# Two interleaved layers on one core: VectorE's exponentials begin in the first layer with the 12th head in place of the 11th

## The chip, the cores and the metric

The kernel runs on one core of a Trainium2 chip. The metric is device time in microseconds of one execution, the median over several runs. The engines are TensorE (matmuls, written PE in the profile, its weight loads PEld), VectorE (DVE), ScalarE (ACT), GpSimd (POOL) and SyncE (SP), which issues nearly all DMAs. Each engine runs its own queue in order and waits on semaphores. Matmul results land in PSUM, which has eight banks of 128 partitions x 512 float32; everything else lies in SBUF or in HBM.

## The reference

Two blocks, each applied twice: multi-head attention with 16 heads of 28 features over 2048 tokens, then a gated MLP, each behind a layer norm and with a residual.

```python
def _A_ref(x, wqkv, wo):
    B, S, D = x.shape                      # 1, 2048, 448
    H = 16; Dh = D // H                    # 28
    qkv = (x @ wqkv).reshape(B, S, 3, H, Dh).transpose(2, 0, 3, 1, 4)
    q, k, v = qkv[0], qkv[1], qkv[2]
    scores = jnp.einsum("bhqd,bhkd->bhqk", q, k) * (Dh ** -0.5)
    p = _softmax(scores, axis=-1)
    o = jnp.einsum("bhqk,bhkd->bhqd", p, v)
    return o.transpose(0, 2, 1, 3).reshape(B, S, D) @ wo

def _B_ref(x, w_gate, w_up, w_down):       # F = 1792
    g = x @ w_gate; u = x @ w_up
    return (_sigmoid(g) * u) @ w_down

x = A_x
x = x + _A_ref(_layernorm(x), A_wqkv, A_wo)
x = x + _B_ref(_layernorm(x), B_w_gate, B_w_up, B_w_down)
x = x + _A_ref(_layernorm(x), A_wqkv, A_wo)
x = x + _B_ref(_layernorm(x), B_w_gate, B_w_up, B_w_down)
```

## The kernel before

Each layer runs in four stages, one after the other: `project` makes queries, keys and values; `attend` does the scores, the exponentials and the sums with the values; `out_project` applies `wo`; `gated` is the MLP. Float32 operands are split into two 16-bit parts for the products. The change lies in `attend` (L831), and only in its first call, that of the first layer.

**Units.** The scores of a head form a 2048 x 2048 matrix. It is cut into 16 chunks of 128 keys, and each chunk into 4 units of 128 keys x 512 queries, so 64 units a head and 1024 a layer. `scores` (L856) computes a unit with four matmuls into one PSUM bank. Unit number `u` belongs to head `u // 64`. Heads are counted from 0 in the code, so "the 11th head" is head 10.

**Two ways to an exponential.** Most units go in threes: `score(g)` fills three banks (`triple`, two sets of three in turn, so six of the eight banks) and ScalarE exponentiates all three in one pass of 128x1536 (L871) into one of six `prob` buffers. These are the `main` units, and `g` counts their groups. In heads from `free_from` on, two units a head take a second way: `score_aside` (L873) computes the unit into a single bank, and VectorE makes the exponential with a polynomial and a shift into the exponent, ten instructions from L881 to L890. The table `side` says which: when the unit at chunk 4 of the head has been scored, the unit of chunk 10, query block 3, is done aside; at chunk 9, that of chunk 15, block 1. `free_from` is 10 in the first layer and 0 in the second.

**Mixing.** `mix` (L907) multiplies the probabilities of a chunk with the values and adds into the head's accumulator, a bank of its own (`acc`). A chunk is mixed in four quarters of 128 queries out of each block. After the last chunk, `finish(h)` (L928) copies the accumulator out on VectorE (L933), divides by the sum of the exponentials (L934 to L936), splits the result (L937, L938) and sends it by DMA to the `ot` tiles.

**The two remaining banks.** The accumulator of head `h` has bank `h % 2`. The side units of head `h` use the bank `1 - h % 2`, which is the one that held the accumulator of head `h - 1`. A matmul of a side unit therefore waits until L933 of `finish(h - 1)` has read that bank.

**The order.** It is written out by hand: a loop over `g` scores group `g`, then does at most one side unit that is due, then mixes as many quarters as the pace says (three a group up to `alone`, the group at which head `free_from` begins; after that `pace`, which counts the side units in). Mixing stays at least two groups behind the scores. TensorE executes this order as it stands:

```python
        for g in range(2, groups + 3):
            more(g)
            x = g - 2.25
            due = int(3 * x if x < alone else 3 * alone + (x - alone) * pace)
            ...
            if begin:
                score_aside(begin.popleft())
                done += 1
            while done < due and i < quarters and last_group[i // 4] <= g - 2:
                ...
                mix(i, n)
```

`more(g)` also fetches the operands of a head two ahead (`HeadOperands.load`: a MEMSET on VectorE at L467 and five loads, and one more for the guard rows) when the ninth unit of a head is scored.

**What else VectorE does in this stage.** In the first layer alone, `Prepare` (L715) measures, scales and splits the weights of `wo`, `w_gate`, `w_up` and `w_down` and writes the parts to HBM for both layers. `along` calls it after every sixth chunk that has been mixed; each step reads the next raw weights, writes out the pack made before, and works on the raw weights that have come (L189 and L194 for the splits). It has 26 steps, after the chunks 6, 12, ... 156. The last lies in head 9.

Of the kernel before, what the change touches and what calls it, by code (L numbers as in the profile page):

```python
# [88 lines left out]
def interleaved_layers(ctx: ExitStack, tc: tile.TileContext, x_in, wqkv, wo, w_gate, w_up,  # L89
# [741 lines left out]
    def attend(layer, values, heads, last_values, gate, keep):  # L831
# [8 lines left out]


        side = {}
        free_from = 10 if layer == 0 else 0
        for h in range(free_from, H):
            for at, kc, qb in ((4, 10, 3), (9, 15, 1)):
                side[(h * NT + at) * NB] = (h * NT + kc) * NB + qb
# [320 lines left out]
    for layer in range(LAYERS):  # L1167
        values, heads, last_values = project(layer, wq, first)
        gate = WeightsGated()
        outs = attend(layer, values, heads, last_values, gate, wq.keep)  # L1170
        mlp_first = out_project(outs, gate)
        wq = WeightsQKV()

        def before_next(f, wq=wq):
            if f == 6:
                wq.load()

        first = gated(layer, mlp_first, gate, before_next)
# [28 lines left out]
```

## Time and profile before

| | us |
|---|---|
| median of 3 runs | 2001.17 (1999.59 to 2002.54) |
| the profiled execution, whole | 2000.05 |
| its span, first to last instruction | 1998.3 |
| TensorE busy | 1965.6 (98%) |
| ScalarE busy | 1167.3 (58%) |
| VectorE busy | 1003.4 (50%) |
| scores of the first layer, first pass of ScalarE to last | 126.1 to 591.8 |
| scores of the second layer, the same | 1124.1 to 1568.2 |
| exponential passes of ScalarE (L871) | 669, busy 898.4 |

The profile is one execution, taken by the hardware profiler. Times inside it count from the start of the span. A row of the timeline has the start, the length, the engine, the line in the kernel, the operation, output and inputs, how many instructions were merged, and in brackets how long the engine had been idle before and what ended that. A row of the list of waits has who waited for whom, the total in us, the number of times and the longest. A row of stretches has for each engine the busy time and the number of instructions (PE, PEld, DVE, ACT, POOL), then the clock granted to TensorE (1.00 is full), the busy share of the DMA engines and the GB/s that they moved. Passes of ScalarE overlap by some tenths of a microsecond, so the length of a row is not the spacing of passes; the busy time of a line is the union of its instructions.

### The profile page before, as it was taken

The numbers are of one execution on the slowest core, as the hardware profiler recorded it, in microseconds if no ns is written. First come the engines' busy times: TensorE is split into PE (matmuls) and PEld (weight loads), VectorE is DVE, ScalarE is ACT, GpSimd is POOL, SyncE is SP. The second block draws the span as 40 slices with busy tenths as digits, with TensorE's granted clock in tenths as the row PEclk, the third lists the DMA queues.
The fourth block names the chain that finished last, engine by engine and source line by source line (L and its number), as shares of the span: only waits on it lengthen the run. The fifth ranks groups of instructions, "written<-read, shape, count | busy, mean of one in ns | idle before, by whom it ended". The sixth has DMA issues, their size and how long they took to land. (4 is left out here: it accounts for less than half of the span.)

```text
span 1998.3 us, 48079 instructions
## 1 busy us (share of the span) xinstructions
PE 1965.6 (98%) x21549; PEld 1001.7 (50%) x21549; DVE 1003.4 (50%) x1551; ACT 1167.3 (58%) x1129; POOL 33.5 (2%) x76
## 2 busy tenths in 40 slices
PE   9999999979999999999999999999999999999999
PEld 4445555545554444444444555555555544444444
DVE  6634545477664323333255477677776732323222
ACT  5569999979981211121235699999999412121211
POOL 2000000000000000000000000000000000000000
PEclk9999999989999999999999999999999999999999
DMA  4563544751016101010234311111111250101000
GB/s 166 161 208 84 149 124 152 224 146 43 17 51 233 37 1 37 1 38 1 92 94 140 100 48 32 48 49 44 46 34 51 68 196 11 56 1 56 0 19 19
DMA packets 98633, 153.77 MB, mean 77 GB/s; under 512 B 9584, under 2 KB 79216, under 8 KB 95600
## 3 DMA queue, kind: packets, MB, share of 16 engines
q1 hardware_dynamic: 89728, 146.21, 23.9%
q10 hardware_dynamic: 8688, 4.36, 0.9%
q8 instruction: 173, 2.83, 0.6%
q14 instruction: 44, 0.36, 0.1%
HBM read 97.52 MB, written 45.68 MB: 72 GB/s over the span
## 5 line engine op out<-in xcount | busy, mean ns | idle before, releaser
L871 ACT ACTIVATE prob_s<-sc 128x1536 f32<-128x1536 f32 x669 | 898.4, 1562 | 15.4 <-PE sc L856 13.0
L907 PE MATMUL acc<-prob_s,val_s 128*32 128x256 f32 (+3 forms) x7938 | 568.1, 381 | 0.0
L856 PE MATMUL sc<-qp_s 114*32 114x512 f16 x8016 | 557.8, 380 | 3.2 <-ACT val_s L567 1.3
L1116 ACT ACTIVATE sig_q<-gate 128x512 f32<-128x512 f32 x112 | 60.8, 595 | 597.4 <-PE up L386 597.4
L856 PEld LDWEIGHTS <-qp_s 114*32 114x32 f16 x8192 | 247.6, 95 | 251.9 <-issue 142.8
L907 PEld LDWEIGHTS acc<-prob_s,val_s 128*32 128x32 f32 x7938 | 263.2, 110 | 155.1 <-issue 9.7
L1117 DVE SCALAR_TENSOR_TENSOR sig_q<-up,sig_q 128x512 f32<-128x512 f32 x112 | 72.1, 686 | 513.8 <-ACT sig_q L1116 513.8
L1080 PE MATMUL dnp<-dn_s,hhl_q 128*128 128x448 f16 x448 | 158.4, 354 | 0.0
L1081 PE MATMUL dnp<-dn_s,hhl_q 128*128 128x448 f16 x448 | 157.9, 352 | 0.0
L1082 PE MATMUL dnp<-dn_s,hhl_q 128*128 128x448 f16 x448 | 157.9, 352 | 0.0
L372 PE MATMUL qkp<-xhl_s,wqk_s 128*128 128x512 f16 x616 | 139.6, 379 | 2.6 <-ACT xhl_s L178 0.9
L379 PE MATMUL gate<-xhl_s,gu_s 128*128 128x512 f16 x336 | 127.3, 379 | 3.4 <-ACT xhl_s L178 2.5
L380 PE MATMUL gate<-xhl_s,gu_s 128*128 128x512 f16 x336 | 127.3, 379 | 1.4 <-DVE xhl_s L179 1.4
L381 PE MATMUL up<-xhl_s,gu_s 128*128 128x512 f16 x336 | 127.3, 379 | 0.0
L380 PE MATMUL up<-xhl_s,gu_s 128*128 128x512 f16 x336 | 127.3, 379 | 0.0
L379 PE MATMUL up<-xhl_s,gu_s 128*128 128x512 f16 x336 | 127.3, 379 | 0.0
L381 PE MATMUL gate<-xhl_s,gu_s 128*128 128x512 f16 x336 | 127.3, 379 | 0.0
L933 DVE COPY oraw_q<-acc 128x512 f32<-128x512 f32 x32 | 22.1, 692 | 179.1 <-PE acc L907 179.0
L935 DVE RECIPROCAL oden_q<-oden_q 128x512 f32<-128x512 f32 x32 | 107.3, 3353 | 1.1
L380 PEld LDWEIGHTS <-gu_s 128*128 128x128 f16 x672 | 65.7, 98 | 81.3 <-issue 3.9
L381 PEld LDWEIGHTS <-gu_s 128*128 128x128 f16 x672 | 65.7, 98 | 81.3 <-issue 2.5
L379 PEld LDWEIGHTS <-gu_s 128*128 128x128 f16 x672 | 65.7, 98 | 79.0 <-issue 1.7
(139 smaller groups left out, 1900.8 us busy)
## 6 DMA issues: line engine op xcount, KB each, us to landing
qp_s<-qk_scr SPq DMA_DIRECT2D x96, 224.0 KB
qk_scr<-qkhl_q SPq DMA_DIRECT2D x56, 256.0 KB
gu_s<-gu_parts SPq DMA_DIRECT2D x14, 1024.0 KB
xraw_s<-xt_scr SPq DMA_DIRECT2D x14, 768.0 KB
xt_scr<-xs_s SPq DMA_DIRECT2D x38, 224.0 KB
qp_s<-qk_scr SPq DMA_DIRECT2D x64, 112.0 KB
gu_parts<-pack_s SPq DMA_DIRECT2D x7, 1024.0 KB
raw_s<-in_B_w_down_dram SPq DMA_DIRECT2D x6, 896.0 KB
```

The source lines that it names most:

```text
L372: nc.tensor.matmul(pm, w, x, start=(i == 0), stop=(i == len(terms) - 1))
L379: nc.tensor.matmul(pm, wh(o, kt), blk.hi[:, kt, :], start=(kt == 0), stop=False)
L380: nc.tensor.matmul(pm, wh(o, kt), blk.lo[:, kt, :], start=False, stop=False)
L381: nc.tensor.matmul(pm, wl(o, kt), blk.hi[:, kt, :], start=False, stop=False)
L856: nc.tensor.matmul(ps[32 * j:32 * j + 32, :], hd.k[:, keys], hd.q[:, qb * W:(qb + 1) * W], start=True, stop=True, tile_position=(0, 32 * j))
L871: nc.scalar.activation(prob[:, 0:n, :], ps[:, 0:n, :], AF.Exp, scale=exp_scale)
L907: nc.tensor.matmul(acc[qb * VC:(qb + 1) * VC, s], v[:, kc % TB, h, :], probs[c * NB + qb][:, s], start=(kc == 0 and a == 0), stop=(kc == N ...
L935: nc.vector.reciprocal(den, den)
L1080: nc.tensor.matmul(pm, hl[:, 0, s], dw[:, 0, :], start=(f == 0), stop=False)
L1081: nc.tensor.matmul(pm, hl[:, 0, s], dw[:, 1, :], start=False, stop=False)
L1082: nc.tensor.matmul(pm, hl[:, 1, s], dw[:, 0, :], start=False, stop=(f == NF - 1))
L1117: nc.vector.scalar_tensor_tensor(sigs[a], pms[2 * a + 1], PS, sigs[a], op0=ALU.mult, op1=ALU.mult)
```

## The change

In the first layer the heads with side units begin with head 11 in place of head 10. Head 10's two side units (12 side units in the layer before, 10 after) become main units, exponentiated by ScalarE. `alone` and `pace` follow: the pace of three quarters a group holds through head 10, and the pace after that goes from 3.176 to 3.192 units of mixing and side work a group. The second layer is not touched.

```diff
@@ -840,7 +840,7 @@
         side = {}
-        free_from = 10 if layer == 0 else 0
+        free_from = 11 if layer == 0 else 0
         for h in range(free_from, H):
             for at, kc, qb in ((4, 10, 3), (9, 15, 1)):
                 side[(h * NT + at) * NB] = (h * NT + kc) * NB + qb
```

## Prediction

> **What bounds the kernel now.** I read the page's busy rows by slice first, then the waits, then the timeline at the one place where both fall, then stretches of the two attention stages.
>
> ```profile
> span 1998.3 us, 48079 instructions
> ...
> PE   9999999979999999999999999999999999999999
> ...
> DVE  6634545477664323333255477677776732323222
> ACT  5569999979981211121235699999999412121211
> ```
>
> TensorE is full in every slice of 50 us but the ninth (400 to 450 us), and ScalarE falls in the same slice. Everywhere else in both attention stages both are full, so time is gained there only in that slice. The waits name it:
>
> ```profile
> PE aside L856 <- DVE oraw_q L933: 10.3, 1, 10.3
> ...
> ACT prob_s L871 <- PE sc L856: 13.0, 5, 11.4
> ```
>
> One wait of TensorE, once, 10.3 us: the first score unit that VectorE is to exponentiate (`aside`) waits for the copy at L933, and ScalarE then waits 11.4 us for TensorE. The reason is PSUM: the `aside` tile of head 10 lies in bank 1, which is head 9's accumulator, and L933 is what empties it. The timeline at that place (start, length, engine, line):
>
> ```profile
> 422.87 0.75 DVE L189 TENSOR_SCALAR pack_s<-raw_s,up 128x1024 f16<-128x1024 f32 x1 [9.60 <-DMA gu_parts<-pack_s]
> ...
> 427.40 1.76 DVE L467 MEMSET qp_s<- 18x2048 f16 x1 [0.48 <-issue]
> ...
> 429.20 0.69 DVE L933 COPY oraw_q<-acc 128x512 f32<-128x512 f32 x1
> ...
> 429.94 0.62 PE L856 MATMUL aside<-qp_s 114*32 114x512 f16 x4 [10.33 <-DVE oraw_q L933]
> ...
> 431.18 1.52 PE L856 MATMUL sc<-qp_s 114*32 114x512 f16 x12
> ...
> 433.52 0.83 PE L856 MATMUL sc<-qp_s 114*32 114x512 f16 x12
> ```
>
> VectorE runs its queue in order. Head 9's sums were complete on TensorE by about 417.4 (the mixing call that holds them starts at 416.75), but VectorE stood in the last weight split of `Prepare`, which itself stood 9.60 us until an earlier pack had been written out. Its L933 came 12 us late, and TensorE, whose queue is in order too, stood at `aside` with every later score and mixing behind it. The 10 us before that (the MEMSET at 400.72 waits 10.30 us for a `gu_parts` write, so head 8's L933 starts at 402.52) cost nothing, since no `aside` existed then.
>
> ScalarE's timeline prices the whole loss:
>
> ```profile
> 408.96 12.46 ACT L871 ACTIVATE prob_s<-sc 128x1536 f32<-128x1536 f32 x9
> 432.81 1.45 ACT L871 ACTIVATE prob_s<-sc 128x1536 f32<-128x1536 f32 x1 [11.39 <-PE sc L856]
> 434.47 8.34 ACT L871 ACTIVATE prob_s<-sc 128x1536 f32<-128x1536 f32 x6 [0.21 <-PE sc L856]
> ```
>
> The ninth pass ends at 421.42, the sixteenth at 442.81: seven passes took 21.39 us. A pass costs 1.343 us (the page's L871 row: 898.4 us over 669 passes), so seven cost 9.40 and **12.0 us are lost**. That is more than the 10.33 of idle TensorE because the clock fell too:
>
> ```profile
> 420.00:423.00 3.00, 0.00 (x0) 0.00 (x0) 0.13 (x1) 1.42 (x2) 0.00 (x0) 1.00 1.01 423
> 423.00:430.00 7.00, 0.06 (x4) 0.05 (x7) 6.37 (x8) 0.00 (x0) 0.00 (x0) 0.50 0.57 209
> 430.00:433.00 3.00, 3.00 (x32) 1.41 (x35) 2.97 (x2) 0.19 (x1) 0.00 (x0) 0.50 0.85 209
> 433.00:436.00 3.00, 3.00 (x60) 1.61 (x56) 2.90 (x5) 2.73 (x3) 0.00 (x0) 0.95 0.73 158
> ```
>
> The third number from the right is the granted clock: half from 423 to about 433. Some 3.3 us of matmuls ran at half speed after the wait (twelve scores took 1.28 us start to next group, against 0.65 later), which is the other 1.6 us.
>
> **The change, part by part.** *Head 10 loses its two side units.* TensorE no longer asks for bank 1 in head 10. The next reader of that bank is head 11's first mixing, some 28 us later, when L933 of head 9 is long done. VectorE's chain up to 436 us hangs on DMAs and on itself, not on the stalled matmuls, so it stays where it is while TensorE and ScalarE go on under it. Gain: 12.0 us.
>
> *VectorE loses 20 instructions*, two chains of ten, each 6.37 us (435.89 to 442.26 for the first), 12.7 us in all. It is busy 110.4 of the 154 us from 436 to 590, off the path: worth nothing.
>
> *The two units go into the main passes.* Main units of this layer go from 1012 to 1014. That is 338 passes either way, the last with one unit before and three after. TensorE's scores and mixings are the same in number. Cost from both sides:
> - Upper: ScalarE as the bound, two thirds of a pass, 2/3 x 1.343 = 0.9 us.
> - Lower: the number of passes does not change, only the end does. From the last score to the out projection this layer takes 3.35 us (590.74 to 594.09) with one unit in its last pass, the second layer 3.57 (1567.17 to 1570.74) with two: 0.22 a unit, 0.43 for two. Against this, 21 passes move from the mixed pace to the pace without side units: 1.343 (110 passes, 441.33 to 589.09) against 1.339 (55 passes, 153.87 to 227.52), 0.1 less. So 0.3.
> - Between: the passes without side units do 6 units of TensorE work each (3 scores, 3 mixed quarters), those with 6.18; 21 x 0.18 x 1.343/6.18 = 0.8 us of TensorE work is put off, less the same 0.1: 0.7.
> A gain is excluded, as nothing gets less on TensorE or ScalarE. I take 0.6.
>
> *The mixing pace* after the switch goes from 3.176 to 3.192 a pass; the second layer runs at 3.190 in 1.343 us a pass: nothing more than is counted.
>
> *Queues.* No DMA is added or taken away; SP's order is the same, its loads and stores after head 9 only carry other buffers, and POOL has nothing in this stage. Head 11's operands were issued from 400.26 to 404.63 and the DMA share is near zero from 407 to 410, so they have landed by then; they are wanted at about 441 instead of 453. Head 12's, issued by 432, are wanted at about 470.
>
> *The next `aside` is head 11's*, in bank 0, behind L933 of head 10. That copy ran at 457.62; 12.0 earlier is 445.6, done by 446.3. The `aside` comes one pass later against it than before (pass 240, the copy in pass 237): 459.75 - 12.0 + 1.34 = 449.1. That is a margin of 2.8 us, where the other heads show 1.0 to 2.3 and never wait. VectorE ends its last late work at 435.98.
>
> **Sum** against the profiled execution (2000.05 us, span 1998.3): -12.0 + 0.6 = -11.4, so 1988.65. The median shown is 1.1 higher than that execution (2001.17); I put half of that on top: **1989.2 us**.
>
> **The rivals.** *A second late copy.* The wait moves to head 11's `aside`. For it: heads 8 and 9 both had their copy late by DMA waits in front of it. Against: `Prepare` has ended, and only the MEMSET for head 13's operands stands before the copy. Even a repeat of the longest DMA wait (10.30) from 436.0 ends at 446.3, MEMSET 1.77 and copy 0.69 later it is 448.8, still before 449.1. A wait of about 5 us would leave 1989.2 + 5 = 1994.
>
> *The busiest engine decides.* The two stretches with passes show ScalarE busy all the time (157.03 of 157.30 us from 433.7 to 591) and VectorE 112.56. If the 12 us came back elsewhere (an input of the out projection that is late anyway), only the added two units on ScalarE would remain: 2000.05 + 0.9 = 2000.95, no change. Against it: in the list of TensorE's waits the next largest after the 10.3 us is 2.5 us (two waits of a gate product for its split input), so no input later in the span is now waited for, and none is near enough to being late to swallow 12 us that come off everything before it alike. [...]
>
> *Slower.* L933 of head 10 is held up longer than that of head 9 was. One wait of VectorE for a DMA in front of the MEMSET does it: it would have to end after 449.1 + 12.0 + 4 - 2.5 = 462.6, so last 26 us from 436.0, for a time 0.2% up, 2004 or more. The longest such wait seen is 10.3.
>
> **How the numbers follow.** As forecast 0.85; second late copy 0.06 (1994); absorbed 0.05 (2001); slower 0.04 (2005). About 0.2% (4 us) is what a measurement of this kernel tells from no change. Faster: 0.85 and most of the second, 0.89; same 0.07; slower 0.04. The range: low 2000.05 - 12.1 + 0.3 - 0.5 (the fastest run is 0.5 under the profiled one), less a margin, 1987.0; high 2000.05 - 11.5 + 0.9 + 2.5 (the slowest run), 1992.0, and 1.0 towards the second late copy: 1993.0.
>
> **What would show it.** In the profile after: the wait of `aside` for L933 gone and the ninth slice full; no half clock between 420 and 435; the copy of head 9 still at about 429, that of head 10 at about 446; 338 passes of ScalarE in this layer at 1.34 us; L881 in 42 instances, not 44; the out projection at about 583 instead of 594.09. It is wrong if `aside` waits for L933 in head 11, if another wait of TensorE appears between 420 and 460, or if the out projection starts early and the end does not move.

## The result, and the profile after

The changed kernel takes 1989.5 us (median of 5 runs, 1988.37 to 1993.31) against 2000.45 before (5 runs); the ratio is 0.9948, with a 95% interval of 0.9933 to 0.9962. It is faster by 0.5%. The forecast was 1989.2, within 1987.0 to 1993.0. The profiled execution after takes 1989.2 us against 2000.05, its span 1987.5 against 1998.3.

The busy rows by slice of the changed kernel, with the row of the granted clock under them:

```profile
span 1987.5 us, 48026 instructions
...
PE   9999999999999999999999999999999999999999
...
DVE  6634545557764332323265477677766732323222
ACT  5569999999971212121135799999999312121111
...
PEclk9999999999999999999999999999999999999999
```

TensorE's ninth slice is full now, ScalarE's too. In the list of TensorE's waits the 10.3 us for L933 is gone, and nothing has taken its place; these are the two longest:

```profile
PE gate L379 <- ACT xhl_s L178: 2.9, 2, 1.9
PE vp L396 <- PEq L674: 2.0, 2, 1.3
```

The timeline of VectorE around the old wait, and the first side unit of head 11:

```profile
420.41 0.75 DVE L189 TENSOR_SCALAR pack_s<-raw_s,up 128x1024 f16<-128x1024 f32 x1 [9.28 <-DMA gu_parts<-pack_s]
...
426.75 0.69 DVE L933 COPY oraw_q<-acc 128x512 f32<-128x512 f32 x1
...
445.30 0.69 DVE L933 COPY oraw_q<-acc 128x512 f32<-128x512 f32 x1 [9.53 <-PE acc L907]
...
448.43 0.40 PE L856 MATMUL aside<-qp_s 114*32 114x512 f16 x4
```

VectorE is nearly as late with head 9's copy as it was: it stands 9.28 us for the write of a pack (9.60 before) and copies at 426.75. Nobody waits for it. Head 10's copy runs at 445.30, the moment its sums are complete, and the side unit that needs the bank comes 2.44 us after the copy has ended. The same four stretches as before show no idle TensorE and a full clock:

```profile
420.00:423.00 3.00, 3.00 (x68) 1.88 (x64) 2.56 (x3) 3.00 (x3) 0.00 (x0) 1.00 0.50 202
423.00:430.00 7.00, 7.00 (x128) 3.54 (x121) 6.37 (x7) 7.00 (x6) 0.00 (x0) 1.00 0.66 201
430.00:433.00 3.00, 3.00 (x64) 1.70 (x57) 2.90 (x4) 3.00 (x4) 0.00 (x0) 1.00 0.87 186
433.00:436.00 3.00, 3.00 (x56) 1.40 (x51) 2.29 (x2) 3.00 (x3) 0.00 (x0) 1.00 0.08 21
```

For all that follows I compare one stretch, "the stage": from the first pass of ScalarE in the first layer (L871) to the first product of the out projection (L396), read from the timeline. Its first and last rows before, and then after, are:

```profile
126.09 2.79 ACT L871 ACTIVATE prob_s<-sc 128x1536 f32<-128x1536 f32 x2 [2.38 <-DMA qp_s<-qk_scr]
...
594.09 0.36 PE L396 MATMUL op<-wout_s,ot_s 128*128 128x448 f16 x1
```

```profile
125.54 2.79 ACT L871 ACTIVATE prob_s<-sc 128x1536 f32<-128x1536 f32 x2 [1.82 <-DMA qp_s<-qk_scr]
...
582.07 0.36 PE L396 MATMUL op<-wout_s,ot_s 128*128 128x448 f16 x1
```

The stage repeats far better than whole runs. Before it is 468.00 us, after 456.54: **11.46 us less**. The second layer's attention, which is not touched, takes 446.68 and 446.70. The two spans differ by less, 10.8 us: the stretch between the two attentions went from 529.97 to 531.26 (it lies between 528.2 and 532.0 in all runs below but one), and the first pass starts 0.55 sooner.

### The profile page after: what moved, and what is told of

The parts are those of the page before. It is cut to its first block, busy times and chain, and to the rows that moved or that the text cites. A ratio compares the mean times of both kernels' runs of the same rounds, so it can differ in the third digit from the quotient of the medians.

```text
span 1987.5 us, 48026 instructions
## 1 busy us (share of the span) xinstructions
PE 1964.1 (99%) x21533; PEld 1003.5 (50%) x21533; DVE 991.6 (50%) x1531; ACT 1168.0 (59%) x1129; POOL 33.3 (2%) x76
## 5 line engine op out<-in xcount | busy, mean ns | idle before, releaser
L871 ACT ACTIVATE prob_s<-sc 128x1536 f32<-128x1536 f32 x669 | 899.0, 1565 | 3.2 <-DMA qp_s<-qk_scr 2.1
L933 DVE COPY oraw_q<-acc 128x512 f32<-128x512 f32 x32 | 22.1, 692 | 180.4 <-PE acc L907 180.3
```

The source lines that it names most:

```text
L871: nc.scalar.activation(prob[:, 0:n, :], ps[:, 0:n, :], AF.Exp, scale=exp_scale)
```

## The experiments

**Is it the late copy, or the side units themselves?** Four kernels tell these apart (e1, e2, e4 and e5 below). The first two leave the side units where they were, or add some, and make `Prepare` end sooner:

```diff
-            if prepare and prepare.steps and c > 4 and c % 6 == 0:
+            if prepare and prepare.steps and c > 4 and c % 5 == 0:
```

> The kernel before, its side units from head 10 on as they were, but Prepare takes a step after every fifth chunk instead of every sixth, so that its last step lies in head 8 and VectorE is no longer late at head 9's copy. Measure: the first layer's attention stage, from the first pass of ScalarE to the first product of the out projection: 468.0 us before, 456.5 after the change. Theory (VectorE's late copy of head 9 held the side unit of head 10): the wait is gone although no unit is moved, stage about 455.9 us (456.5 less the 0.6 that the pair costs on ScalarE and TensorE), whole about 1988.9 us. Rival (the pair of side units itself is what costs, through VectorE's work or the shared bank): the pair is still there, stage about 468 us, whole about 2000.5 us.

Measured: 1994.45 us, ratio 0.9967 (0.9954 to 0.9981); the stage is 460.14. The side unit of head 10 no longer waits, though both units are still there. The stage is 4.2 us longer than expected, because VectorE is now late one head sooner, so late that the next user of head 7's bank is stopped, the first mixing of head 9 (TensorE's waits, then its timeline):

```profile
PE acc L907 <- DVE oraw_q L933: 2.6, 1, 2.6
```

```profile
389.63 0.41 PE L907 MATMUL acc<-prob_s,val_s 128*32 128x128 f32 x8
392.66 0.64 PE L907 MATMUL acc<-prob_s,val_s 128*32 128x256 f32 x8 [2.62 <-DVE oraw_q L933]
```

ScalarE's passes lose 4.4 us there (start to start, over 1.343 a pass). Without them the stage would be 455.8, and 455.9 was expected.

With the same edit and `free_from = 9` (e2):

> The same earlier Prepare, and side units from head 9 on. Theory: no late copy in front of head 9's side unit either (Prepare ends at chunk 130, the copy of head 8 comes at chunk 143), and one more pair saves 0.3 to 0.9 us: stage about 455.3 us, whole about 1988.3 us. Rival (a pair costs by itself): one pair more than before, so some 11 us slower than before, 2011 us.

Measured: 2000.08 us, ratio 0.9993 (0.9982 to 1.0003), no change; stage 465.00. The forecast missed: the late copy is now that of head 8, and head 9's side unit waits for it. (Head 9's first mixing waits 1.5 us as well, for the copy of head 7.) ScalarE's passes lose 10.1 us there; without them the stage would be 454.9, and 455.3 was expected.

```profile
PE aside L856 <- DVE oraw_q L933: 6.5, 1, 6.5
```

Both misses have one cause: I placed the end of `Prepare` by its last step, and not by how far VectorE lags behind its steps. At one step every five chunks it lags by more than a head, which takes 28.5 us: the copy of head 7 starts at 391.91 in the first of these kernels, and TensorE's last product of that head ends at 360.91, 31.0 us sooner. The rival falls all the same: with one pair more than before the stage is 3 us shorter, not 11 longer.

The third (e4) puts the changed kernel's `Prepare` off by one head, so that its last steps stand before head 10's copy:

```diff
-            if prepare and prepare.steps and c > 4 and c % 6 == 0:
+            if prepare and prepare.steps and c > 20 and (c - 16) % 6 == 0:
```

> The changed kernel (side units from head 11), with all 26 steps of Prepare put off by 16 chunks, one head: its last two steps stand before the copy of head 10 as they stood before the copy of head 9. Theory: the wait comes back, now at head 11's first side unit, with about the same length: stage about 468 us, whole about 2000.9 us. Rival (fewer side units are what gained): units are those of the changed kernel, stage 456.5 us, whole 1989.5 us.

Measured: 2010.64 us, ratio 1.0044 (1.0032 to 1.0056); stage 479.30. The wait is back at head 11, with the changed kernel's own side units, and twice as long. Its waits, then VectorE's timeline:

```profile
PE aside L856 <- DVE oraw_q L933: 20.4, 1, 20.4
```

```profile
457.62 0.75 DVE L189 TENSOR_SCALAR pack_s<-raw_s,up 128x1024 f16<-128x1024 f32 x1 [15.31 <-DMA gu_parts<-pack_s]
...
468.05 0.69 DVE L933 COPY oraw_q<-acc 128x512 f32<-128x512 f32 x1
```

The write that VectorE waits for stands in SyncE's queue behind the stores of head 9. Those are eight and not four, as head 9's features lie in two `ot` tiles, and SyncE issues them from 442.34 to 448.49 before the next loads (to 452.1) and the write. That the stores make up the whole of the further 10 us I did not test.

The fourth (e5) leaves everything in place and lets TensorE come to head 10's side units later:

```diff
-            for at, kc, qb in ((4, 10, 3), (9, 15, 1)):
+            places = ((7, 13, 3), (11, 15, 1)) if layer == 0 and h == 10 else ((4, 10, 3), (9, 15, 1))
+            for at, kc, qb in places:
```

> The kernel before, with head 10's two side units scored later in the head, at chunks 7 and 11 instead of 4 and 9 (they are then the units of chunks 13 and 15). Nothing else moves. Theory: TensorE reaches the side unit three chunks later, 3 x 4/3 x 1.343 = 5.4 us, so it waits about 5 us instead of 10.3, the clock still falls; 6.6 us lost instead of 12.0: stage about 462.6 us, whole about 1995.1 us. Rival (the number of side units decides): stage 468 us, whole 2000.5 us.

Measured: 1997.59 us, ratio 0.9976 (0.9964 to 0.9989); stage 462.66, against 462.6 expected. TensorE's wait (the edit shifts the lines by one):

```profile
PE aside L857 <- DVE oraw_q L934: 4.2, 1, 4.2
```

This is the cleanest of the four: as many units on the same engines, only asked for later (5.5 us, counted from the first pass), and 5.34 us less in the stage. That this meets the forecast to 0.1 us is partly luck. The wait fell by 6.2 us, as the copy came 0.7 sooner too, but the half clock behind it lasted longer (430.30 to 435.24, against 429.94 to 433.29 before), which at half speed costs 0.8 us more, an estimate from these two lengths.

**What a pair of side units is worth.** The changed kernel again, and one with `free_from = 15` (e3):

> The changed kernel once more, beside the three below on one chip. First attention stage 456.5 us as before, whole about 1989.5 us, and the copy of head 9 again at about 427 us with nobody waiting for it.

Measured: 1989.02 us, ratio 0.9944 (0.9927 to 0.9960); stage 456.48, head 9's copy at 427.5 with no one behind it.

> Side units in the first layer from head 15 on: four heads more than in the changed kernel give their pair to ScalarE's passes, and nobody waits for VectorE. Theory (a pair on VectorE saves a little, 0.3 to 0.9 us, of which 0.8 by the stage of e1 less its gaps): stage 457.7 to 460.1 us, 459.6 by the 0.8, whole about 1992.6 us. Rival (side units cost by themselves, so that fewer are better): under 456.5 us.

Measured: 1991.74 us, ratio 0.9957 (0.9943 to 0.9971); stage 461.25, above the 457.7 to 460.1 expected. Of that, 1.07 us lie between the first two passes and the third, where nothing differs in the code: the granted clock was half there, from 125.30 to 128.72, and it was full in the changed kernel. The other 3.64 us over 456.54 are 0.91 for each of four pairs: ScalarE's two thirds of a pass, 0.895, nearly to the figure. Side units on VectorE are worth something, and fewer are not better.

**Why VectorE is late.** Two ways to free it, with the side units from head 10 on as before. One large buffer more, which serves the packs too (e6):

```diff
-N_SLOTS = 19
-N_QUART = 12
+N_SLOTS = 20
+N_QUART = 8
```

> The kernel before with 20 large buffers in place of 19, and 8 small ones in place of 12 to make room. What made VectorE late is open between two: (a) a buffer still being written out to HBM is taken again at once, as there are too few; (b) SyncE's queue issues the writes late, behind stores that wait for VectorE. By (a) the waits of 10.3 and 9.6 us for writes to gu_parts shrink, the copy of head 9 comes at about 418 us, the side unit does not wait: stage about 455.8 us, whole about 1989 us. By (b) both waits stay: stage 468 us, whole 2000.5 us. The fewer small buffers may add waits of VectorE for the stores of a finished head, later in a head, with no one behind them.

Measured: 1993.35 us, ratio 0.9961 (0.9947 to 0.9975); stage 457.81, with 1.75 us of that again before the third pass (half clock from 131.72 to 135.13); without them it would be 456.06, near the 455.8 of (a). The whole misses the 1989 expected because in its profile the first pass starts at 131.43, 5.3 us later than before and ahead of the stage; whether the fewer small buffers cause that I did not test. Another queue for the writes (e7):

```diff
-                nc.sync.dma_start(*self.pack[0:2])
+                nc.gpsimd.dma_start(*self.pack[0:2])
```

> The kernel before with the writes of Prepare's packs issued by GpSimd's queue, which is empty in this stage, in place of SyncE's. By (b), SyncE's order as the cause: a write starts when its pack is ready (the pack of 390.4 at once and not at 395.3; that of 413.3 at once and not behind the stores of head 8), the copy of head 9 comes 5 to 12 us earlier, stage 456 to 463 us, whole 1989 to 1996 us. By (a), too few buffers alone: stage 468 us, whole 2000.5 us.

Measured: 1990.19 us, ratio 0.9954 (0.9937 to 0.9970); stage 456.02. VectorE's timeline, of the kernel with 20 buffers and then of that with the writes on GpSimd's queue:

```profile
418.84 1.76 DVE L467 MEMSET qp_s<- 18x2048 f16 x1 [1.58 <-DMA gu_parts<-pack_s]
424.52 0.69 DVE L933 COPY oraw_q<-acc 128x512 f32<-128x512 f32 x1 [3.91 <-PE acc L907]
```

```profile
412.71 1.76 DVE L467 MEMSET qp_s<- 18x2048 f16 x1 [0.48 <-issue]
418.26 0.69 DVE L933 COPY oraw_q<-acc 128x512 f32<-128x512 f32 x1 [3.79 <-PE acc L907]
```

In both, head 9's copy waits for TensorE and not the other way round. So neither half alone made VectorE late: a pack's buffer is wanted again at once, and its write leaves SyncE late; taking away either is enough. With the writes on GpSimd the stage is 0.52 us shorter than the changed kernel's, with head 10's pair still on VectorE: about what that pair is worth in the changed kernel, if the other queue itself costs nothing.

**Can more side units be had that way?** GpSimd's queue for the writes, and side units from heads 8, 5 and 0 on (in the last two, in heads before 10, the units of chunks 12 and 15, scored at chunks 4 and 8):

> Prepare's packs written from GpSimd's queue, side units from head 8 on. With the writes there, VectorE copied the heads 7, 8 and 9 as soon as TensorE had them, so nobody should wait; two pairs more than with head 10, 0.5 to 0.9 us each: stage 454.2 to 455.0 us against 456.0, whole about 1988.8 us. If VectorE's waits for raw weights (6.6 us in head 8) hold a side unit's result, TensorE waits in the mixing and the stage is over 456 us.

> The same with side units from head 5 on; in the heads before 10 they are the units of chunks 12 and 15, scored at chunks 4 and 8, so that VectorE has longer. Five pairs more than with head 10: stage 451.5 to 453.5 us if VectorE keeps up beside Prepare, whole about 1987 us; over 456 us if it does not.

> The same with side units in all heads of the first layer. Ten pairs more than with head 10: stage 447 to 451 us if VectorE keeps up (the second layer, which has them in all heads and no Prepare, takes 446.7), whole about 1982 to 1985 us; over 456 us if waits for raw weights hold the copies or the results of side units.

Measured: 1989.7 us (stage 456.72), 2005.54 (464.28) and 2001.2 (466.36). All three missed. New waits take more than the pairs bring. From head 8 on they are 1.2 us for a late copy and 1.2 for VectorE's reading of the first side unit; from head 0 on, TensorE's waits read:

```profile
PE aside L857 <- DVE expo_q L882: 7.5, 3, 3.2
PE aside L857 <- DVE oraw_q L934: 6.0, 2, 5.1
```

The kernel with head 5 has a shorter stage than before and is 0.2% slower as a whole (ratio 1.0020, 1.0010 to 1.0030); that from head 0 on is no change (0.9993, 0.9982 to 1.0003). The one with head 5 takes 536.0 us between the two attentions, with one wait of TensorE of 4.5 us among the second layer's values for which the profile names no cause. What causes it is open. No version tried beats the changed kernel by more than the runs can tell: the writes on GpSimd with head 10 (0.9954) or head 8 (1989.7 us, ratio 0.9938, 0.9922 to 0.9955) stand beside its 0.9948.

## Why the prediction was right

*The bound and the wait.* The chain L933 late, bank held, `aside` stopped, everything behind it stopped, is shown by e5 (later request, less loss), e4 (late VectorE put back, wait back) and e7 (VectorE on time, no wait with the units unmoved).

*The gain, 12.0 us.* The prediction took it from ScalarE's passes, with the half clock in it, and not from the 10.33 us of the wait list. The most direct check is e7, which takes the wait away and leaves every unit in place: its stage is 11.98 less than before. In the changed kernel the stage fell by 11.46. Added back, the longer end (0.43) and the passes after head 10, which come every 1.345 us and no longer every 1.343 (110 passes, 0.2), make 12.1.

*The cost, 0.3 to 0.9, taken at 0.6.* The end of the stage is the part that can be read directly: from the start of the last pass to the out projection 2.32 us before (591.77 to 594.09), 2.76 after (579.32 to 582.07), 0.43 more, the figure forecast. The whole is 0.52 by e7's stage. For pairs beyond this one it is 0.91: the changed kernel's two units filled a last pass that was two thirds empty, so its 338 passes stayed 338, while `free_from = 15` needs 341. The upper end of the range was the price of the next pairs, not of this one.

*What stays late.* The prediction said that VectorE's chain up to 436 us hangs on DMAs and not on the stalled TensorE, so that it would stay. The copy moved from 429.20 to 426.75; the repetition had 427.5, and `free_from = 15` 429.73. Of the 2.45 us, 2.15 were there already at head 8's copy (402.52 to 400.37), ahead of anything that the change moves, so this is scatter and not an effect of the change.

*The next side unit.* Forecast: copy done at 446.3, request at 449.1. Measured: 445.99 and 448.43, margin 2.44 where 2.8 was said. The out projection was forecast at about 583 and starts at 582.07.

*The rivals.* The second late copy did not come in the changed kernel, but it is real: e1, e2 and e4 are three ways to it, and of these e4 alone made the kernel slower. One wait of 26 us for a DMA was said to be needed for a slower kernel; with `Prepare` put off, 15.3 us did it. The wait began at 442.31 and not at 436.0, and four weight splits (8.2 us) came between it and the MEMSET, which the forecast had excluded since `Prepare` had ended. The time named for the MEMSET, 462.6, was passed (466.26). Of the rival of the busiest engine only the smaller term came, more work on ScalarE: 0.9 us was taken for it from the passes of this case, and e3 has 0.91 a pair. The gap, 11.39 us on ScalarE before, did not come back elsewhere.

*The sum.* 11.4 us were forecast, 11.46 came in the stage and 10.8 in the span, whose other stretches scatter by more than the difference. That the whole came within 0.3 us of the forecast is luck in part: single runs of the changed kernel lie between 1988.37 and 1993.31, and the 0.55 us put on top of the sum was a compromise between the profiled execution and the median before.

## What to carry to other kernels

Look at what the last buffer of a side job stands behind, not only at how busy its engine is: VectorE was half empty (50% busy), but in order, and a store waiting in another queue held up the one copy that TensorE needed. Here a request moved to behind a late engine's copy was worth more (12.0 us) than the work that moved with it cost (0.5), and a late copy that had no one behind it cost nothing, so first find who asks first. Price a stall by the passes that did not start: here they were worth 12.0 us, for a wait of 10.33 us with the granted clock at half (0.50) until 433.29.

## What the runs showed of the hardware

In these runs the granted clock also fell beside waits far shorter than the 10.3 us of this case. In e1 TensorE stood 2.62 us (390.04 to 392.66), began again at full clock (1.00 from 392.70 to 393.80), and was then at half for 3.4 us. The stretches (the third number from the right is the clock):

```profile
390.00:392.60 2.60, 0.04 (x4) 0.00 (x0) 2.46 (x2) 1.62 (x2) 0.00 (x0) 1.00 0.01 2
392.70:393.80 1.10, 1.10 (x24) 0.62 (x28) 1.06 (x2) 0.00 (x0) 0.00 (x0) 1.00 0.24 74
393.90:397.20 3.30, 3.30 (x40) 1.59 (x32) 3.27 (x2) 2.10 (x2) 0.00 (x0) 0.50 0.18 47
397.30:399.00 1.70, 1.70 (x32) 0.81 (x28) 1.31 (x3) 1.37 (x2) 0.00 (x0) 1.00 0.00 0
```

ScalarE's passes lost 4.4 us there, for that wait of 2.6. The same shows before the first product of the first MLP, some 34 us into the stretch between the attentions, where TensorE waits for its split input: in the changed kernel it stood 1.87 us there and kept its clock (1.00 from 617.4 to 621.0), in its repetition 2.04 us and was at half from 618.8 to 622.2.

The order is not that of the lengths: in e3 there was half clock from 125.30 to 128.72 beside a wait of 1.56 us ahead of the first passes (123.98 to 125.53), which is shorter than the 1.87 us at which the changed kernel kept its clock. What decides it was not shown.
